# Block attention into a gelu MLP on one core: attention steps 13 to 17 in three batches instead of five

## The chip, the core and the metric

The kernel runs on one core of one Trainium2 chip. The metric is the device time of one execution in microseconds. Before the change it is 199.8 us, the median of three runs (199.78 to 200.85). The profile of one execution has a span of 198.3 us, and that run took 200.1 us, so about 1.8 us of a run lie outside the profiled span.

Names used below: PE is the TensorE, DVE the VectorE, ACT the ScalarE, POOL the GpSimd engine; SP is the engine whose queue starts nearly all transfers.

## The reference, cut to what matters

A causal attention with a per-head decay, computed in blocks of 64 positions with a running 64x64 state per head, and on its output a two-layer MLP with a tanh gelu. Batch 4, 8 heads, 768 positions, head size 64; 3072 tokens of width 512, hidden width 2048.

```python
for b in range(nb):                       # 12 blocks of 64 positions
    intra = einsum('bhic,bhjc->bhij', qb, kb) * Dmask
    intra = einsum('bhij,bhjd->bhid', intra, vb)
    inter = einsum('bhid,bhde->bhie', qb * lam_pow, kv_state)
    out[:, :, sl] = intra + inter
    kv_state = lam_block * kv_state + einsum('bhsd,bhse->bhde', kb * rev_pow, vb)
x = out.transpose(0, 2, 1, 3).reshape(3072, 512)
h = x @ w_in
g = 0.5 * h * (1 + tanh(c * (h + 0.044715 * h**3)))
result = g @ w_out
```

## The kernel before: the parts that the change touches

The attention is cut into 24 steps. A step is 256 positions (a super-block) of four of the eight heads: steps 2m and 2m+1 are the two head halves of super-block m, and three super-blocks make one batch entry. The MLP takes the super-blocks in seven groups, `[[0, 1], [2], [3], [4, 5], [6, 7], [8, 9], [10, 11]]`. Group 3 holds steps 8 to 11, group 4 steps 12 to 15, group 5 steps 16 to 19.

The work of a group is put as small pieces into a list, the filler, when its last attention step has been evacuated. One piece of group 3 is four matmuls of 512 columns with their gelu on ACT, or one of the later products of 8 or 16 smaller matmuls. `fill(n)` issues the next n pieces. So PE alternates between attention steps and runs of MLP pieces, and the program order on every engine is pinned to the order of the calls.

The pools that count here:

```python
ld   = tile_pool(name="ld", bufs=4)      # q, k, v as loaded, fp32
a16p = tile_pool(name="a16", bufs=5)     # q and k in one fp16 tile, v in another
qkp  = tile_pool(name="qkp", bufs=4)     # q and k transposed
ptp  = tile_pool(name="ptp", bufs=3)     # masked scores
ps_M = tile_pool(name="psM", bufs=8, space=PSUM)   # every PSUM tile, one tag
```

Preparing a step: a cast of q times its decay on DVE, a cast of k on ACT, a transpose of both by DMA from SP (from step 9 on), a cast of v on POOL, and then the loads of the step three further on.

```python
def prep_qk(s):
    q32, k32, _ = ld32[s]
    tqk = a16p.tile([P, 2, 2, HH, D], FP16, tag="qk16", ...)
    ...
    pin(q_eng.tensor_tensor(wide(tq), q32[:], decay(dq, s), ALU.mult))   # DVE
    ...
    pin(nc.scalar.activation(out=wide(tk), in_=k32[:], func=AF.Copy))    # ACT
    a16[s] = (tq, tk)
    if s >= FIRST_DMA_T:
        o = qkp.tile([P, 2, 2, 2, P], FP16, tag="qkT", ...)
        pin(nc.sync.dma_start_transpose(out=o..., in_=tqk...))           # SP
        qkT[s] = o
        ...

def prep_v(s):
    tv = a16p.tile([P, 2, HH, D], FP16, tag="v16", ...)
    pin(nc.gpsimd.tensor_tensor(wide(tv[:]), ld32[s][2][:], decay(dv, s), ALU.mult))
    ...
    if s >= 6:
        ...load_ahead(s + 3)                 # q, k, v of step s+3, from SP

def prep(s):
    prep_qk(s)
    prep_v(s)
```

A single step: `R(n, s)` takes the scores of step n (S, 16 matmuls in 64x64 tiles of PE, from the transposed q and k), its keys times values (K, 16 matmuls in 64x64 tiles, 8 in the last super-block of a batch entry), the output of the earlier step s (O, 16 matmuls in 64x64 tiles from the masked scores, and 2 or 4 full-size matmuls with the state u, here called U matmuls). Then ACT copies the output into the MLP's input xT, DVE masks the scores of n, and DVE and POOL advance the state. It takes four PSUM tiles, two for S and two that O and K share (the tiles OK).

```python
def R(n, s, ahead=None):
    if n is not None: scores(n)          # S: 16 matmuls
    if ahead: ahead()
    products(n, s)                       # K: 16 or 8; O: 16; U: 2 or 4; x_out(s) on ACT
    if n is not None: causal(n)          # DVE: PT = S * mask, two instructions
    ...                                  # queue_group when s closes a group
    if n is not None: update(n, 0)       # DVE t, POOL u
def U(n): update(n, 1)                   # the second half of the state update
```

A batch: `burst(ns, ss)` does the same for several steps at once, ordered by kind of matmul. For two steps n it takes all eight PSUM tiles: four S, two O, two K.

```python
def burst(ns, ss, *mix):
    for n in ns: scores(n)
    O = [ps_M.tile([P, 2, 2, P], FP32, tag="M", ...) for c in range(2)]
    for i, s in enumerate(ss): ...       # 16 matmuls O <- PT, v for each s
    K = [ps_M.tile([P, 2, P], FP32, tag="M", ...) for c in range(2)]
    for i, n in enumerate(ns): ...       # 16 or 8 matmuls K <- v, qk for each n
    for i, s in enumerate(ss): ...       # 2 or 4 matmuls O <- qkT, u for each s
    for n in ns: causal(n)
    for i, s in enumerate(ss): x_out(s, ...)
    ...
    if i == len(groups[g]) - 1:
        queue_group(g, *mix)
    for n in ns: update(n, 0)
```

The schedule before: steps 8 to 17 one at a time, and from 18 on in pairs. `sum_win` is one of eight DVE sums of quarters of the first weight matrix, used from about 135 us on.

```python
FILL = {8: (0, 2, 1, 2), ..., 12: (0, 2, 1, 3),
        13: (0, 2, 1, 3), 14: (0, 3, 1, 3), 15: (0, 2, 1, 3), 16: (0, 2, 1, 3), 17: (0, 3, 1, 3)}
for n, (a, b, c, d) in FILL.items():
    stage_t(n)                 # nothing for n >= 9
    fill(a)
    prep_qk(n + 2) if n == 8 else prep(n + 2)
    fill(b)
    R(n, n - 1)
    fill(c)
    U(n)
    ...
    if n == 17:
        prep_qk(20); fill(1); prep_qk(21); fill(1); prep_v(20); prep_v(21); fill(1)
    else:
        fill(d)
    if 8 < n < 17:
        sum_win((n - 7) // 2, (n - 1) % 2, nc.vector)
burst((18, 19), (17,))
fill(2); U(18); U(19); fill(4); prep_qk(22); fill(2)
burst((20, 21), (18, 19), 11, 4)
...
```

Of the kernel before, what the change touches and what calls it, by code (L numbers as in the profile page):

```python
# [15 lines left out]
def kernel(  # L16
# [10 lines left out]
    nc = tc.nc  # L27
# [108 lines left out]
    def w_in_block(t, cs, fs):  # L136

        if t in I_SUMS:
            return wi_sum[(t - 1) // 2][:, (t - 1) % 2, cs, fs]
        F, C = t  # L140
        return w_in16[:, 2 * C + cs.start : 2 * C + cs.stop,
                      F * DFF // 2 + fs.start : F * DFF // 2 + fs.stop]

    def sum_win(m, j, eng):

        if not wi_sum:
            wi_sum.extend(wst.tile([P, 2, 2, DFF // 2], FP16, tag=f"w{2 + i}", name=f"ws{i}")
                          for i in range(2))
        a, op, b = I_SUMS[m]
        cs, fs = slice(0, 2), slice(512 * j, 512 * j + 512)  # L150
        pin(eng.tensor_tensor(w_in_block(m, cs, fs), w_in_block(a, cs, fs),
                              w_in_block(b, cs, fs), op))
# [17 lines left out]
    def load_ahead(s):  # L170
        if s < NSTEP:
            load_step(s)
# [50 lines left out]
    def odd(hs):  # L223
        pin(nc.vector.tensor_tensor(dq[:, hs, 1], dq[:, hs, 0], lam_bc[:, hs], ALU.mult))

    def inverse(hs):
        pin(nc.vector.reciprocal(dv[:, hs], dq[:, hs]))
# [17 lines left out]
# [4 lines that stand above are left out]
    def wide(t):  # L249
        return t.rearrange("p j h d -> p h j d")  # L250

    def decay(t, s):
        hs = halves[s % 2]
        return t[:, hs, :].unsqueeze(3).to_broadcast([P, HH, 2, D])

    def prep_v(s):
        tv = a16p.tile([P, 2, HH, D], FP16, tag="v16", name=f"v16_{s}")
        pin(nc.gpsimd.tensor_tensor(wide(tv[:]), ld32[s][2][:], decay(dv, s), ALU.mult))  # L258
        a16[s] = a16[s] + (tv,)
        if s >= 6:  # L260
            if s + 3 == FIRST_DMA_T + 1:
                load_step(s + 3, "qk")
            else:
                load_ahead(s + 3)

    def prep_qk(s):
        q32, k32, _ = ld32[s]
        tqk = a16p.tile([P, 2, 2, HH, D], FP16, tag="qk16", name=f"qk16_{s}")
        tq, tk = tqk[:, 0], tqk[:, 1]
        q_eng = nc.gpsimd if s == 3 else nc.vector  # L270
        pin(q_eng.tensor_tensor(wide(tq), q32[:], decay(dq, s), ALU.mult))  # L271
        if s == 0:
            inverse(halves[0])
            odd(halves[1])
            inverse(halves[1])
        pin(nc.scalar.activation(out=wide(tk), in_=k32[:], func=AF.Copy))  # L276
        a16[s] = (tq, tk)
        if s >= FIRST_DMA_T:
            o = qkp.tile([P, 2, 2, 2, P], FP16, tag="qkT", name=f"qkT_{s}")
            pin(nc.sync.dma_start_transpose(out=o[:].rearrange("p a j h t -> p (a j h) t"),  # L280
                                            in_=tqk[:].rearrange("p a j h d -> p (a j h d)")))
            qkT[s] = o
            if s == FIRST_DMA_T:
                load_step(s + 1, "v")
# [31 lines left out]
    def half64(i):  # L316
        return slice(64 * i, 64 * i + 64)
# [74 lines left out]
    def burst(ns, ss, *mix):  # L392


        for n in ns:
            scores(n)
        O = [ps_M.tile([P, 2, 2, P], FP32, tag="M", name=f"O{c}") for c in range(2)]
        seen = set()

        def start(kind, c, hl):  # L400
            new = (kind, c, hl) not in seen
            seen.add((kind, c, hl))
            return new

        qTs = [qkT.pop(s) for s in ss]
        for i, s in enumerate(ss):
            PT, tv = PTs.pop(s), a16.pop(s)[2]
            for hp in range(2):
                for jk in range(2):
                    for c, hl in TILES:  # L410
                        pin(nc.tensor.matmul(
                            O[c][half64(hl), i, hp, :], tv[half64(c), jk, 2 * hp + hl, :],
                            PT[half64(c), hl, hp, jk, :], start=start("O", c, hl), stop=False,
                            skip_group_check=True))
        if ns:
            K = [ps_M.tile([P, 2, P], FP32, tag="M", name=f"K{c}") for c in range(2)]
        for i, n in enumerate(ns):
            _, tk, tv = a16[n]
            last = (n // 2) % NSB == NSB - 1
            for jk in range(2):  # L420
                for hp in range(2):
                    for c, hl in TILES:
                        if c == 1 and last:
                            continue
                        pin(nc.tensor.matmul(
                            K[c][half64(hl), i, hp * D : hp * D + D],
                            tk[half64(c), jk, 2 * hp + hl, :], tv[half64(c), jk, 2 * hp + hl, :],
                            start=start("K", c, hl), stop=(jk == 1), skip_group_check=True))
            Kps[n] = [t[:, i] for t in K]
        for i, s in enumerate(ss):  # L430
            for c in range(2):
                if c == 0 and (s // 2) % NSB == 0:
                    continue
                u = us.pop((s, 0) if c else (s - 2, 1))
                for hp in range(2):
                    pin(nc.tensor.matmul(O[c][:, i, hp, :], u[:, hp].rearrange("p l d -> p (l d)"),  # L436
                                         qTs[i][:, 0, :, hp, half64(c)], start=False, stop=True,
                                         skip_group_check=True))
        for n in ns:
            causal(n)  # L440
        for i, s in enumerate(ss):
            x_out(s, [t[:, i].rearrange("p h t -> p (h t)") for t in O])
        sbg = ss[-1] // 2
        g, i = group_of[sbg]
        if i == len(groups[g]) - 1:
            queue_group(g, *mix)
        for n in ns:
            update(n, 0)
# [59 lines left out]
    groups = [[0, 1], [2], [3], [4, 5], [6, 7], [8, 9], [10, 11]]  # L508
# [3 lines left out]
    def queue_group(g, lead=0, per_set=0):  # L512
# [69 lines left out]
        def product(m, p, part=None):  # L582
# [34 lines left out]
            def out_tile(T):  # L617
                if f"o{T}" not in st:
                    st[f"o{T}"] = otp.tile([P, NP, 2, HE], FP32, tag="o32", name=f"o{T}")
                return st[f"o{T}"]  # L620
# [4 lines left out]
            def store(T, ps=slice(0, NP), es=slice(0, 2)):  # L625
                r = row0 + T * HN
                rows = out[r : r + HN, :].rearrange("(p q) (e d) -> q p e d", q=P, e=2)
                whole = g == 3 or (g, T) == (4, 0)
                for i in [ps] if whole else [slice(i, i + 1) for i in range(ps.start, ps.stop)]:
                    pin(nc.sync.dma_start(out=rows[:, i, es], in_=out_tile(T)[:, i, es, :]))  # L630

# [223 lines left out]
    def fill(n):  # L855
        for _ in range(min(n, len(filler))):
            filler.pop(0)()

    def R(n, s, ahead=None):

        if n is not None:
            scores(n)
        if ahead:
            ahead()
        products(n, s)
        if n is not None:
            causal(n)
        if s is not None and s % 2 == 1:
            g, i = group_of[s // 2]
            if i == len(groups[g]) - 1 and g > 0:  # L870
                queue_group(g)
        if n is not None:
            update(n, 0)

    def U(n):
        update(n, 1)
# [17 lines left out]
    idle(2)  # L894
    stage_t(2)
    prep_qk(3)
    update(1, 0)
    update(1, 1, "t")
# [41 lines left out]
    for m in W_SUMS:  # L940
# [29 lines left out]
    prep_v(9)  # L970
    fill(2)

    FILL = {8: (0, 2, 1, 2), 9: (2, 2, 1, 2), 10: (0, 1, 1, 3), 11: (0, 2, 1, 2), 12: (0, 2, 1, 3),
            13: (0, 2, 1, 3), 14: (0, 3, 1, 3), 15: (0, 2, 1, 3), 16: (0, 2, 1, 3), 17: (0, 3, 1, 3)}
    for n, (a, b, c, d) in FILL.items():
        stage_t(n)
        fill(a)
# [4 lines that stand above are left out]
        U(n)  # L982
        if n == 8:
            prep_v(n + 2)
        if n == 17:
            prep_qk(20)
            fill(1)
            prep_qk(21)
            fill(1)
            prep_v(20)  # L990
            prep_v(21)
            fill(1)
        else:
            fill(d)
        if 8 < n < 17:
            sum_win((n - 7) // 2, (n - 1) % 2, nc.vector)

    burst((18, 19), (17,))
    fill(2)
    U(18)  # L1000
    U(19)
# [47 lines left out]
```

## Time and profile before

| | |
|---|---|
| median of three runs | 199.8 us |
| span of the profiled execution | 198.3 us |
| PE busy | 191.9 us (97%) |
| DVE busy | 151.8 us (77%) |
| ACT busy | 123.0 us (62%) |
| POOL busy | 73.6 us (37%) |

The page of a profile gives the busy time of each engine, the span in 40 slices, and the chain of work that ended last: from the last instruction back, at each step to what released it or to what stood before it on its engine. Where a stretch of that chain is PE alone, PE set the pace there. The chain can also be listed in order of time, each piece with its start, its length, its engine and line and the number of instructions. The timeline lists the instructions of an engine with their start and duration, and in brackets the idle time before them with what ended it. The transfers have a time from issue to landing.

Where the steps stand in time, from the starts of the S matmuls in that chain: R(12, 11) at 81.06 us, R(13, 12) at 87.28, R(14, 13) at 94.24, R(15, 14) at 100.35, R(16, 15) at 106.62, R(17, 16) at 113.75, the batch of 18 and 19 at 118.22, that of 20 and 21 at 126.59.

### The profile page before, as it was taken

Reading aid. Unit: us, or ns where it says so; the run is one execution under the profiler, and the core shown is the slowest. Engines: PE = TensorE matmul, PEld = TensorE weight load, DVE = VectorE, ACT = ScalarE, POOL = GpSimd, SP = SyncE. Lnnn points to the kernel's source line nnn. Section 1 sums busy time; section 2 is a strip of 40 time slices with the busy share of each in tenths; the row PEclk is TensorE's granted clock in tenths of the full one; section 3 lists DMA queues with packets and bytes.
Section 4 is the critical chain, followed back from the end, with each engine's and each line's share of the span. In section 5 each row is a group of like instructions: output and inputs, shape, how many; then the busy total and the mean of one; then the engine's idle time right before and its main releaser. Section 6 shows DMA issues by size and latency. Waiting matters only on the chain.

```text
span 198.3 us, 5936 instructions
## 1 busy us (share of the span) xinstructions
PE 191.9 (97%) x2437; PEld 139.7 (70%) x2439; DVE 151.8 (77%) x296; ACT 123.0 (62%) x251; POOL 73.6 (37%) x85
## 2 busy tenths in 40 slices
PE   8879999999999999999999999999999999999993
PEld 2546544456887888754588755578888888888883
DVE  4887722789989989949899378999678997588720
ACT  3673878466693675577745486754668835778321
POOL 6594223456456652436433565047002030002000
PEclk9999999999999999999999999999999999999999
DMA  6999999999999999999864999320211200020205
GB/s 171 291 324 386 386 386 387 292 289 295 293 297 257 217 293 215 210 317 219 226 142 104 271 286 214 106 56 0 53 37 72 105 9 0 0 108 1 106 3 212
DMA packets 61706, 37.86 MB, mean 191 GB/s; under 512 B 17520, under 2 KB 54640, under 8 KB 61680
## 3 DMA queue, kind: packets, MB, share of 16 engines
q1 hardware_dynamic: 61136, 37.23, 71.8%
q8 instruction: 19, 0.31, 0.7%
q10 hardware_dynamic: 544, 0.26, 0.5%
q14 instruction: 7, 0.06, 0.1%
HBM read 27.26 MB, written 6.29 MB: 169 GB/s over the span
## 4 chain that ended last, share of the span: by engine, by line
PE 88%; SPq 4%; DMA 4%; ACT 1%; issue 1%
PE Hps L529 24%; PE MX L606 17%; PE MY L606 9%; PE HX L698 7%; PE O2ps L544 7%; PE MW L606 4%; DMA wi<-in_moe_w_in_dram 4%; SPq L70 4%; PE HY L698 4%; PE S L327 3%; PE Hps L789 3%; PE OK L385 2%; PE HW L698 2%; PE OK L376 2%; PE Tps L298 1%; PE O L436 1%
## 5 line engine op out<-in xcount | busy, mean ns | idle before, releaser
L529 PE MATMUL Hps<-xT,w_in 128*128 128x512 f16 (+1 forms) x288 | 51.0, 332 | 0.0
L488 POOL TENSOR_TENSOR u<-t,lumask 128x256 f16<-128x256 f32 x40 | 29.6, 752 | 49.7 <-DVE t L481 34.1
L529 PEld LDWEIGHTS <-w_in 128*128 128x128 f16 x288 | 27.8, 98 | 18.8
L533 ACT ACTIVATE gT<-Hps 128x512 f16<-128x512 f32 x56 | 32.9, 597 | 10.3 <-PE Hps L529 9.8
L337 DVE TENSOR_TENSOR PT<-S,mask 128x512 f16<-128x512 f32 x48 | 30.5, 682 | 7.4 <-PE S L327 7.3
L606 PEld LDWEIGHTS <-gs 128*128 128x128 f16 x320 | 31.1, 98 | 4.0 <-DVE gs L576 0.4
L258 POOL TENSOR_TENSOR v<-v,dv 128x512 f16<-128x512 f32 x24 | 29.9, 1249 | 7.3 <-DMA v<-in_v_dram 6.9
L606 PEld LDWEIGHTS <-gT 128*128 128x128 f16 x240 | 23.2, 98 | 3.5 <-ACT gT L533 0.5
L606 PE MATMUL MX<-w_sum,gs 128*128 128x256 f16 x160 | 21.5, 273 | 0.0
L271 DVE TENSOR_TENSOR qk<-q,dq 128x512 f16<-128x512 f32 x23 | 19.1, 835 | 1.1 <-DMA q<-in_q_dram 1.0
L576 DVE TENSOR_TENSOR gs<-gT 128x1024 f16<-128x1024 f16 (+1 forms) x24 | 18.4, 772 | 1.6 <-ACT gT L533 1.6
L276 ACT ACTIVATE qk<-k 128x512 f16<-128x512 f32 x24 | 15.0, 626 | 6.9 <-DMA k<-in_k_dram 6.7
L651 POOL TENSOR_TENSOR o<-u,q 128x512 f32<-128x512 f32 (+1 forms) x5 | 5.4, 1082 | 37.2 <-ACT u L623 37.2
L462 ACT ACTIVATE xT<-OK 128x256 f16<-128x256 f32 x34 | 13.0, 454 | 6.3 <-PE OK L385 6.0
L544 PE MATMUL O2ps<-w_out,gT 128*128 128x512 f16 x64 | 14.6, 379 | 0.0
L698 PEld LDWEIGHTS <-ws 128*128 128x128 f16 x128 | 12.5, 98 | 1.8
L623 ACT ACTIVATE u<-MX 128x256 f32<-128x256 f32 x18 | 6.9, 384 | 10.1 <-PE MX L606 10.1
L481 DVE SCALAR_TENSOR_TENSOR t<-t,lamu,OK 128x64 f32<-128x64 f32 x48 | 11.0, 274 | 1.4 <-issue 0.5
L327 PEld LDWEIGHTS <-qkT 64*64 64x64 f16 x384 | 6.1, 106 | 7.1 <-issue 3.4
L544 PEld LDWEIGHTS <-gT 128*128 128x128 f16 x64 | 6.1, 98 | 6.6
L606 PE MATMUL MY<-w_out,gs 128*128 128x256 f16 x80 | 10.7, 273 | 0.0
L606 PE MATMUL MX<-w_sum,gT 128*128 128x256 f16 x80 | 10.4, 273 | 0.0
(95 smaller groups left out, 311.6 us busy)
## 6 DMA issues: line engine op xcount, KB each, us to landing
q<-in_q_dram SPq DMA_DIRECT2D x24, 256.0 KB, 5.0
k<-in_k_dram SPq DMA_DIRECT2D x24, 256.0 KB, 5.1
v<-in_v_dram SPq DMA_DIRECT2D x23, 256.0 KB, 5.4
out_dram<-o SPq DMA_DIRECT2D x17, 256.0 KB, 4.1
wo<-in_moe_w_out_dram SPq DMA_DIRECT2D x4, 1024.0 KB, 9.5
wi<-in_moe_w_in_dram SPq DMA_DIRECT2D x4, 512.0 KB, 8.0
wi<-in_moe_w_in_dram SPq DMA_DIRECT2D x2, 1024.0 KB, 12.7
out_dram<-o SPq DMA_DIRECT2D x3, 512.0 KB, 5.0
```

What stands on the lines that cost most here:

```text
L258: pin(nc.gpsimd.tensor_tensor(wide(tv[:]), ld32[s][2][:], decay(dv, s), ALU.mult))
L271: pin(q_eng.tensor_tensor(wide(tq), q32[:], decay(dq, s), ALU.mult))
L276: pin(nc.scalar.activation(out=wide(tk), in_=k32[:], func=AF.Copy))
L337: pin(nc.vector.tensor_tensor(t[:, hl].rearrange("p b c d -> p b (c d)"), Sps[:].rearrange("p b c d -> p b (c d)"), mask[:].unsqueeze(1).t ...
L462: pin(nc.scalar.activation(out=d, in_=o, func=AF.Copy))
L488: pin(nc.gpsimd.tensor_tensor(u[:], state[half][:].unsqueeze(2).to_broadcast([P, 2, 2, D]), lumask[:, 2 * half : 2 * half + 2, :].unsqueez ...
L529: pin(nc.tensor.matmul(by_block(Hps[:, i, :]), w_in16[:, c, f * P : (f + 1) * P], x(c), start=(c == 0), stop=(c == NC - 1)))
L533: pin(nc.scalar.activation(out=dst, in_=Hps[:], func=AF.Gelu_apprx_tanh))
L544: pin(nc.tensor.matmul(O2[tau][0][:], gT[:, f % HF, f // HF, tau * P : (tau + 1) * P], w_out16[:, f, :], start=(n == 0), stop=(n == NF - 1)))
L576: pin(nc.vector.tensor_tensor(g_rows(m, i), g_rows(a, i), g_rows(b, i), op))
L606: pin(nc.tensor.matmul(dst, lhsT, rhs, start=(opens and i == 0), stop=(closes and i == HF - 1), skip_group_check=True))
L698: pin(nc.tensor.matmul(dst[:, i, :], w_in_block(a, slice(c, c + 1), slice(f * P, f * P + P))[:, 0], x_block(b, slice(c, c + 1))[:, 0], sta ...
```

## The change

The five calls R(13, 12) to R(17, 16) and the batch (18, 19) with output 17 become three batches and one single step: burst (13, 14) with output 12, burst (15, 16) with outputs 13 and 14, R(17, 15), and burst (18, 19) with outputs 16 and 17. It is for fewer changes of PE between MLP matmuls and attention matmuls. The number of filler pieces between R(12, 11) and the batch of 18 and 19 stays 36.

Since step 16 is now wanted soon after step 14, its casts of q and k are made before the first batch. Its transpose needs the place of step 12's transposed tile (four places, steps 12 to 15 hold them), which is read until the end of that batch, and so is issued after it. The last four weight sums on DVE move behind R(17, 15). One store that was a single transfer of 512 KB becomes two of 256 KB.

```diff
     def prep_qk(s):
+        cast_qk(s)
+        transpose_dma(s)
+
+    def cast_qk(s):
         ...
         a16[s] = (tq, tk)
+        whole_qk[s] = tqk
+
+    whole_qk = {}
+
+    def transpose_dma(s):
+        tqk = whole_qk.pop(s)
         if s >= FIRST_DMA_T:
         ...
-        if i == len(groups[g]) - 1:
+        if ss[-1] % 2 == 1 and i == len(groups[g]) - 1:
             queue_group(g, *mix)
         ...
-                whole = g == 3 or (g, T) == (4, 0)
+                whole = g == 3
         ...
-    FILL = {8: ..., 12: (0, 2, 1, 3),
-            13: (0, 2, 1, 3), 14: (0, 3, 1, 3), 15: (0, 2, 1, 3), 16: (0, 2, 1, 3), 17: (0, 3, 1, 3)}
+    FILL = {8: ..., 12: (0, 2, 1, 3)}
     for n, (a, b, c, d) in FILL.items():
         ...
-        if n == 17:
-            ...
-        else:
-            fill(d)
-        if 8 < n < 17:
+        fill(d)
+        if n > 8:
             sum_win((n - 7) // 2, (n - 1) % 2, nc.vector)
 
-    burst((18, 19), (17,))
+    prep(15)
+    fill(1)
+    cast_qk(16)
+    fill(1)
+    burst((13, 14), (12,))
+    transpose_dma(16)
+    fill(1)
+    U(13)
+    U(14)
+    prep_v(16)
+    fill(6)
+    burst((15, 16), (13, 14))
+    fill(1)
+    U(15)
+    U(16)
+    prep(17)
+    fill(8)
+    prep(18)
+    R(17, 15)
+    fill(1)
+    U(17)
+    fill(1)
+    sum_win(3, 0, nc.vector)
+    fill(2)
+    prep(19)
+    sum_win(3, 1, nc.vector)
+    fill(2)
+    sum_win(4, 0, nc.vector)
+    fill(2)
+    sum_win(4, 1, nc.vector)
+    fill(2)
+    prep_qk(20)
+    fill(1)
+    prep_qk(21)
+    prep_v(20)
+    fill(3)
+
+    burst((18, 19), (16, 17))
+    prep_v(21)
     fill(2)
     U(18)
     U(19)
```

More of the change, by code (lines that the diff above doesn't have):

```diff
@@ L971 @@
     fill(2)
-    FILL = {8: (0, 2, 1, 2), 9: (2, 2, 1, 2), 10: (0, 1, 1, 3), 11: (0, 2, 1, 2), 12: (0, 2, 1, 3),
-            13: (0, 2, 1, 3), 14: (0, 3, 1, 3), 15: (0, 2, 1, 3), 16: (0, 2, 1, 3), 17: (0, 3, 1, 3)}
+    FILL = {8: (0, 2, 1, 2), 9: (2, 2, 1, 2), 10: (0, 1, 1, 3), 11: (0, 2, 1, 2), 12: (0, 2, 1, 3)}
     for n, (a, b, c, d) in FILL.items():
@@ L984 @@
             prep_v(n + 2)
-        if n == 17:
[L986 to L992, printed above, removed]
-        else:
-            fill(d)
-        if 8 < n < 17:
-            sum_win((n - 7) // 2, (n - 1) % 2, nc.vector)
-    burst((18, 19), (17,))
+        fill(d)
+        if n > 8:
+            sum_win((n - 7) // 2, (n - 1) % 2, nc.vector)
+    prep(15)
[36 more added lines that the diff above has]
+    prep_v(21)
     fill(2)
```

## The prediction

> **What bounds the kernel now.** I read the page first, for the engine that fills the span:
>
> ```profile
> span 198.3 us, 5936 instructions
> PE 191.9 (97%) x2437; PEld 139.7 (70%) x2439; DVE 151.8 (77%) x296; ACT 123.0 (62%) x251; POOL 73.6 (37%) x85
> PE 88%; SPq 4%; DMA 4%; ACT 1%; issue 1%
> ```
>
> PE is busy for 97% of the span and makes 88% of the chain that ended last. A busy PE can hide waits, so I went on to the chain in order of time (start, length, what), for the stretch that the change rewrites. First one single step, R(13, 12), with the filler run behind it; then the two batches that exist already:
>
> ```profile
> 87.28 0.35 PE S L327 x16
> 87.63 0.12 PE OK L362 x16
> 87.75 0.23 PE OK L376 x16
> 87.98 0.22 PE OK L385 x2
> 88.19 6.04 PE Hps L529 x28
> ...
> 118.22 0.57 PE S L327 x32
> 118.80 0.22 PE O L411 x16
> 119.02 0.33 PE K L425 x32
> ...
> 126.59 0.57 PE S L327 x32
> 127.16 0.45 PE O L411 x32
> 127.60 0.28 PE K L425 x32
> 127.88 0.33 PE O L436 x4
> ```
>
> The pieces join without a gap, and 28 matmuls in 6.04 us is 0.216 us each, the rate of the long runs everywhere. So between 81 and 128 us PE waits for nothing: time can be won here only by giving PE less to do, and any new wait of PE is lost in full. The lines also price the steps. The first 16 S cost 0.35 us, the next 16 only 0.22: 0.13 is the price of entering. Two U matmuls cost 0.22 and four 0.33: 0.055 each and 0.11 of entering. O and K show hardly any such part.
>
> Then the things that PE could come to wait for. ACT just ahead of R(13, 12) (start, duration), the SP queue behind it (start, issue time), and landings of a load of v and of the transpose of step 16:
>
> ```profile
> 86.08 0.62 ACT L276 ACTIVATE qk<-k 128x512 f16<-128x512 f32 x1
> 86.60 1.31 ACT L533 ACTIVATE gT<-Hps 128x512 f16<-128x512 f32 x2
> ```
> ```profile
> 86.73 2.16 SPq L280 DMA_TRANSPOSE qkT<-qk  x1
> 88.94 0.57 SPq L70 DMA_DIRECT2D q<-in_q_dram  x1
> 89.56 0.51 SPq L70 DMA_DIRECT2D k<-in_k_dram  x1
> 90.11 1.14 SPq L70 DMA_DIRECT2D v<-in_v_dram  x1
> 92.83 1.24 SPq L280 DMA_TRANSPOSE qkT<-qk  x1
> ```
> ```profile
> v<-in_v_dram SPq DMA_DIRECT2D x1, 256.0 KB, 5.0
> qkT<-qk SPq DMA_TRANSPOSE x1, 3.2
> ```
>
> ACT finishes the last gelu before R(13, 12) at 87.91, 0.63 us after PE has begun the step; the single step does not need that bank. The SP queue is busy from 86.73 to 91.25 with the transpose of step 15 and the loads of step 18. The v of step 18 lands at 90.11 + 5.0 = 95.1 us, the transpose of step 16 at 92.83 + 3.2 = 96.0.
>
> **What the Trainium skill says.** "TensorEngine Tiling (Array Packing)", section Key Properties: changing the tiling mode drains TensorE. That is the entering cost that batches share, and the trace agrees (0.13 us at S, 0.11 at U). "TensorE: Matmul & The Clock Gate", section Architectural detail, calls ACT and DVE strict FIFO: a cast put before a gelu delays the gelu and the bank it frees. The trace agrees: the gelus start at 86.60, when the cast of k is through. "DMA: Bandwidth & Descriptors", section Queues, rings and completion order: on each DMA engine a queue's descriptors are consumed in ring order, though writes may finish out of order. So a transpose issued behind three loads mostly lands behind them. The trace agrees for step 16 (96.0 after 95.1).
>
> **What the change saves on PE.** No matmul is added or removed: 112 S, 96 O and all K and U stay. Before, from the chain: R(13, 12) and R(14, 13) 0.91 us each (two U), R(15, 14) 1.03, R(16, 15) and R(17, 16) 1.02 each (four U), the batch of 18 and 19 with one output 1.46 (118.22 to the next MLP piece at 119.68). Sum 6.35. After, put together from the lines above:
> - burst (13, 14) with output 12: S 0.57, O 0.22, K 0.28, two U 0.22, sum 1.29.
> - burst (15, 16) with outputs 13 and 14: S 0.57, O 0.45, 24 K about 0.23, six U 0.44, sum 1.69.
> - R(17, 15): 1.02.
> - burst (18, 19) with outputs 16 and 17: S 0.57, O 0.45, K 0.28, eight U 0.55, sum 1.85.
>
> Together 5.85, and so 0.5 us less. Six visits become four, and each visit saved is 0.13 + 0.11 = 0.24 us, which also gives 0.48. I take 0.45, since the 0.33 of K in the first batch may recur.
>
> **What it may cost: a PSUM bank in the first batch.** Two steps in a batch take all eight banks, so the last one, of K, is the bank of the filler piece just ahead of the batch, and frees when ACT has made its gelu. The cast of k of step 16 now stands between the last two gelus. From their lines a gelu occupies ACT about 0.49 us and a cast of k 0.52 (86.08 to 86.60). So: gelu 86.60, cast 87.09, last gelu 87.61 to 88.21, instead of 87.91. PE reaches K at 87.28 + 0.57 + 0.22 = 88.07. Wait: 0.14, with the signal about 0.17 us.
>
> **What it may cost: the transpose of step 16.** It must wait for the end of the first batch, at about 87.28 + 1.29 + 0.17 = 88.74, but SP reaches it only after the loads of step 18, at 91.3. PE wants it early: seven filler pieces at 0.864 make 6.05, so burst (15, 16) starts at 94.79, and the S of step 16 stands at 94.79 + 0.35 = 95.14. If the transpose lands 3.1 us after its issue, the shortest in the trace, it is there at 94.4 and costs nothing. If it follows the v of step 18 at the same distance of 0.9 us as before, it lands at 96.0 and PE waits 0.8. I take the middle, 0.4.
>
> **What I count as hidden.** DVE: at 91.6 us it is through the four masks (2.48 us for four, at the batch of 18 and 19, from 87.67) and the state updates of 13 and 14 (about 1.3), then the four gelu sums of 0.69 bring it to 94.4, before the next scores at 95.1. It fits only because the weight sum of 0.72 us that stood here is moved, and moving it costs nothing: the sums are read from about 135 us. POOL: four state products of about 0.8 and the cast of v of step 16, 1.49, end near 95.1, and K of step 16 comes near 96. The transposes of steps 20 and 21 both wait now for the end of the third batch (near 120), and by the 3.4 us that the second took before they land by 125.5; their S stands at 126.5 or later. Two stores for one is 0.5 us of SP.
>
> Sum: -0.45 + 0.17 + 0.4 = +0.1 us, so 199.9.
>
> **The rivals.** First, everything new is hidden: the transpose lands by 95.1 and the gelu in time. For it: the issue-to-landing time of transposes in an empty queue is 3.1 to 3.2 us, and the change takes care to make the casts of step 16 early. Against it: three loads stand directly ahead. It makes 199.8 - 0.45 = 199.35. Second, the transpose is a new wait in full: 0.8 to 1.5 us, the latter with a landing 5.5 us after issue, like that of step 15 (5.7). For it: every transpose issued right behind loads here took 4.4 us or more. It makes 200.3 to 201.0. Third, DVE becomes the bound: with two steps' masks and updates at once plus the gelu sums, it holds back the scores' banks and so the MLP pieces. Against it: the addition above, with 0.7 us to spare. For it: that addition has DVE never waiting between 87.7 and 94.4. Half a microsecond more, and the effect would be seen at the seventh piece after a batch; it makes 200.3.
>
> **Range and chances.** The saving is sure to within 0.1 us; the waits run from 0 to about 1.5. With a scatter of runs of some 0.3 us I predict 199.9 us, and 199.3 to 200.7 for 8 times in 10. That the change moves the time by over 2% (4 us) either way I hold for nearly excluded, as it touches some 6 us of PE's time: faster 0.005, within 2% 0.985, slower 0.01.
>
> **What would show it.** In the profile after: the four visits near 1.3, 1.7, 1.0 and 1.85 us in the chain; an ACT gelu ahead of K in the first batch as a wait of 0.1 to 0.3; between the first and the second half of S in burst (15, 16) a wait for the transpose of step 16, landing between 94.4 and 96.5, with the issue at 91.3. No PE wait on DVE or POOL from 88 to 118, and none for the transposes of 20 and 21. I am wrong if the visits do not get shorter, if SP gets to the transpose much earlier or later than 91.3, or if waits appear after 97 us.

## The result, and the profile after

The changed kernel takes 201.76 us (median of six runs, 201.29 to 202.40), against 199.82 for the kernel before: a ratio of 1.009, with a 95% interval of 1.0066 to 1.0115. It is slower by about 1.9 us; I had predicted 199.9 with 200.7 as the upper end.

The page of the changed kernel, the same three lines as before:

```profile
span 200.1 us, 5935 instructions
PE 192.3 (96%) x2437; PEld 140.6 (70%) x2439; DVE 153.8 (77%) x296; ACT 122.8 (61%) x251; POOL 73.6 (37%) x85
PE 86%; DMA 6%; DVE 2%; ACT 2%; issue 1%; SPq 1%; POOL 1%; DVEq 0%; POOLq 0%
```

The busy time of PE tells nothing: 192.3 us, as much as before. The chain tells it. DMA has 6% of it now, and one transfer stands in the middle of the stretch that was pure PE. The chain in order of time (start, length, what), from the first batch on; the second block is the list of PE's waits (total, times, longest), two of its lines. Hps is the first product of an MLP piece and gT its gelu; MX, MY and MW are later MLP products, gs is a DVE sum of gelu tiles, PT are the masked scores:

```profile
87.34 0.52 ACT qk L280
87.85 0.50 ACT gT L543
88.35 0.04 issue
88.39 0.44 PE K L435 x31
88.83 0.22 PE O L446 x2
89.05 2.40 PE Hps L539 x12
91.45 5.49 DMA qkT<-qk
96.94 0.04 issue
96.98 0.42 PE S L337 x16
97.40 0.45 PE O L421 x32
97.85 0.25 PE K L435 x24
98.09 0.44 PE O L446 x6
98.54 3.45 PE Hps L539 x16
...
119.56 0.57 PE S L337 x32
...
121.38 6.91 PE Hps L539 x32
128.29 0.57 PE S L337 x32
```
```profile
PE S L337 <- DMA qkT<-qk: 1.5, 1, 1.5
PE K L435 <- ACT gT L543: 0.2, 1, 0.2
```

Two waits are to be seen, both of the predicted kind. In the first batch K waits for a gelu that ACT could only make after the cast of k of step 16 (the 0.52 ahead of it). In the second, the S of step 16 waits for its transpose, and the two halves of S cost 0.35 and 0.42 us where a joint S costs 0.57: PE pays the entering twice, some 0.2 us. Where the transfer comes from is in the SP queue (start, issue time) and in the landings (the last number, us from issue):

```profile
89.02 0.58 SPq L70 DMA_DIRECT2D q<-in_q_dram  x1
89.64 0.51 SPq L70 DMA_DIRECT2D k<-in_k_dram  x1
90.19 1.09 SPq L70 DMA_DIRECT2D v<-in_v_dram  x1
91.45 1.56 SPq L290 DMA_TRANSPOSE qkT<-qk  x1
```
```profile
v<-in_v_dram SPq DMA_DIRECT2D x1, 256.0 KB, 5.7
qkT<-qk SPq DMA_TRANSPOSE x1, 5.5
```

SP issues the transpose at 91.45, behind the three loads of step 18. The v of step 18 lands at 90.19 + 5.7 = 95.9, the transpose 1.0 us after it, at 96.9. In the kernel before they landed at 95.1 and 96.0, although the transpose was issued 1.4 us later: issuing it earlier behind the same loads brought nothing.

The account of the stretch from R(12, 11) to the batch of 20 and 21: 81.06 to 126.59, 45.53 us, before; 81.21 to 128.29, 47.08, after. So 1.55 us arise here, of the 1.8 by which the two spans differ. The four visits take 1.62, 3.44, 1.02 and 1.82 us, in all 7.90 against 6.35.

### The profile page after: what moved, and what is told of

Read it like the earlier page. It is cut to its first block, busy times and chain, and to the rows that moved or that the text cites. A ratio compares the mean times of both kernels' runs of the same rounds, so it can differ in the third digit from the quotient of the medians.

```text
span 200.1 us, 5935 instructions
## 1 busy us (share of the span) xinstructions
PE 192.3 (96%) x2437; PEld 140.6 (70%) x2439; DVE 153.8 (77%) x296; ACT 122.8 (61%) x251; POOL 73.6 (37%) x85
## 4 chain that ended last, share of the span: by engine, by line
PE 86%; DMA 6%; DVE 2%; ACT 2%; issue 1%; SPq 1%; POOL 1%; DVEq 0%; POOLq 0%
PE Hps L539 21%; PE MX L616 17%; PE MY L616 9%; PE HX L708 7%; PE O2ps L554 7%; PE MW L616 4%; PE Hps L799 4%; PE HY L708 4%; DMA v<-in_v_dram 3%; PE S L337 3%; DMA qkT<-qk 3%; PE HW L708 2%; PE OK L395 2%; PE Tps L308 1%; PE O L446 1%; PE OK L386 1%
## 5 line engine op out<-in xcount | busy, mean ns | idle before, releaser
L586 DVE TENSOR_TENSOR gs<-gT 128x1024 f16<-128x1024 f16 (+1 forms) x24 | 17.2, 723 | 4.2 <-ACT gT L543 4.2
L275 DVE TENSOR_TENSOR qk<-q,dq 128x512 f16<-128x512 f32 x23 | 20.1, 882 | 0.3 <-DMA q<-in_q_dram 0.3
L472 ACT ACTIVATE xT<-OK 128x256 f16<-128x256 f32 x26 | 9.9, 452 | 8.3 <-PE OK L395 8.2
L472 ACT ACTIVATE xT<-O 128x256 f16<-128x256 f32 x22 | 8.0, 460 | 7.7 <-PE O L446 7.1
L337 PE MATMUL S<-qkT 64*64 64x128 f16 x384 | 9.3, 222 | 2.1 <-DMA qkT<-qk 1.5
L586 DVE TENSOR_TENSOR gs<-gs,gT 128x1024 f16<-128x1024 f16 (+1 forms) x12 | 11.1, 923 | 0.3
```

The lines of the kernel that those rows point to most:

```text
L337: pin(nc.tensor.matmul(Sps[hl][half64(c), hp, jk, :], o[half64(hl), 1, jk, hp, half64(c)], o[half64(hl), 0, :, hp, half64(c)], start=True, ...
L472: pin(nc.scalar.activation(out=d, in_=o, func=AF.Copy))
L586: pin(nc.vector.tensor_tensor(g_rows(m, i), g_rows(a, i), g_rows(b, i), op))
```

## The experiments

Theory A: the saving on PE is there, and is lost to the transpose of step 16, which is late because of its place behind the loads of step 18, and a little to the gelu behind the cast. Rivals: B, the transpose is late because it waits for the place that step 12 frees, or is slow anywhere; C, DVE holds PE back as soon as the transfer does not. All edits are to the changed kernel unless said otherwise. In eleven of E5's 22 runs and three of E8's seven the clock of the core was lower (0.991 to 0.992), and the times given for these two leave those runs out; all other medians hold every run.

**E1: the loads of step 18 behind the transpose of step 16.**

```diff
-        if s >= 6:
+        if s >= 6 and s != 15:             # prep_v(15) loads nothing
     ...
     transpose_dma(16)
+    load_ahead(18)
```

> The changed kernel with the three loads of step 18 issued behind the transpose of step 16 instead of ahead of it; nothing else moves. Theory A (the new wait is the place of the transpose in the transfer queue): the transpose is issued near 89.1 us, when the first batch ends, lands by 93.5, the wait of 1.54 us between the two halves of S and the 0.2 us of entering S a second time go, and the time falls from 201.76 to about 200.0; the wait of K for the gelu (0.3 us) stays. Rival B (the transpose waits mostly for the slot that the first batch frees, or takes 5.5 us anywhere): it lands at 94.6 or later and the time falls by at most 0.5 us. Rival C (DVE's work holds back the scores once the transpose does not): the wait for the transpose goes, but waits of PE on DVE of 0.5 us or more take its place, time 200.5 to 201.3.

Measured: 200.14 us, ratio to the kernel before 1.0017 (1.0009 to 1.0025). So 1.6 us of the loss go with the order of four transfers. The transpose is issued at 88.80 instead of 91.45, and PE waits for it no more:

```profile
88.80 2.19 SPq L290 DMA_TRANSPOSE qkT<-qk  x1
```

Its landing is not recorded, but its packets are. Every transpose here moves 1024 packets of 256 bytes, and the last of these ends at 92.52 us, 3.7 us after the issue. So the transpose is not slow wherever it stands, which was one half of rival B. Rival C showed itself too, in a small way. The chain of E1 around the second batch:

```profile
91.86 1.15 DVE gs L586
93.01 0.02 issue
93.03 1.43 DVE gs L586
94.46 0.02 issue
94.48 1.29 DVE gs L586 x2
95.78 0.61 DVE PT L347
96.39 0.04 issue
96.43 3.61 PE Hps L539 x16
```

DVE is at its four gelu sums until 95.78, then makes the first mask of step 15, and the MLP piece behind the batch starts 0.04 us after that mask has freed its bank; its 16 matmuls take 3.61 us instead of 3.45. It costs some 0.2 us, which the late transfer had covered up.

**E2: the casts of steps 15 and 16 one filler piece earlier.**

```diff
-    FILL = {..., 12: (0, 2, 1, 3)}
+    FILL = {..., 12: (0, 2, 1, 2)}
     prep(15)
-    fill(1)
     cast_qk(16)
-    fill(1)
+    fill(3)
     burst((13, 14), (12,))
```

> The changed kernel with the casts of steps 15 and 16 made one filler piece earlier, both together, so that ACT can catch up before the first batch. Theory A: the wait of K for the last gelu (0.3 us) goes, but the transpose of step 16 still lands near 96.9, so PE only waits longer for it (1.8 instead of 1.54 us) and the time stays at 201.6 to 201.9. Rival B (the two waits add): 201.4 or less.

Measured: 201.67 us, ratio 1.0099 (1.0064 to 1.0134). K of the first batch waits no more. But the wait for the transpose is 1.50 us in the trace, not the 1.8 expected: with the casts of step 15 earlier, SP starts earlier too, and the transpose of step 16 lands at 96.67, 0.27 before its time in the changed kernel. The stretch from R(12, 11) to the batch of 20 and 21 is 46.76 us against 47.08. The medians differ by only 0.09 us, but each is of six runs that spread over 1 us or more; whether the edit alone gains 0.3 us or nothing stays open, and rival B is not excluded. In both traces PE goes on 0.04 us after the landing. Two lines of the chain of E2:

```profile
88.27 0.33 PE K L435 x32
...
91.09 5.58 DMA qkT<-qk
```

**E3: both edits.**

> Both edits together: loads of step 18 behind the transpose of step 16, and the casts of steps 15 and 16 one filler piece earlier. Theory A: both waits go, 1.54 + 0.2 + 0.3 us, and what is left is the saving of the shorter visits: 201.76 - 2.05 = 199.7, or 199.35 if the 0.3 us outside the rewritten stretch are noise of the profile. That is 0 to 0.5 us under the kernel before. Rival C (DVE): 200.2 or more with waits of PE on DVE.

Measured: 199.85 us, ratio 0.9993 (0.9973 to 1.0012): the kernel before, not better. The edit of E2 is worth 0.29 us here (200.14 to 199.85), and the stretch agrees (45.58 us in E1, 45.30 here). The wait on the mask is as in E1 (the MLP piece starts at 96.42, again with 3.61 us).

**E4: nine MLP pieces between the first two batches instead of seven.**

```diff
     prep_v(16)
-    fill(6)
+    fill(8)
     burst((15, 16), (13, 14))
     ...
     prep(17)
-    fill(8)
+    fill(6)
     prep(18)
```

> The changed kernel with two of the MLP pieces moved from behind the second batch to ahead of it (9 pieces between the first two batches instead of 7); the transfers keep their order. Theory A: the second batch comes 1.73 us later on PE, near 96.8, the transpose still lands near 96.9, the wait of 1.54 us shrinks to 0 to 0.3, and the time is 200.0 to 200.3, as with the loads behind the transpose. Rival B (something other than the landing sets the second batch): the wait moves along with the batch, time 201.3 or more.

Measured: 200.95 us, ratio 1.0055 (1.0027 to 1.0082), with runs from 199.93 to 202.72. The wait for step 16's transpose fell to 0.20 us in the profiled run, whose span was 198.5 us, as theory A has it; this is PE there:

```profile
96.42 0.42 PE L337 MATMUL S<-qkT 64*64 64x128 f16 x16
97.03 0.42 PE L337 MATMUL S<-qkT 64*64 64x128 f16 x16 [0.20 <-DMA qkT<-qk]
```

But the median missed the expected 200.0 to 200.3. In the same trace the S of step 17 comes just as its transpose lands, 101.3 + 3.4 = 104.7 us. The two pieces taken from behind the second batch are missing there as time for step 17. Two landings on the edge would also explain the wide scatter; the longer runs have no trace, so that is argued, not shown.

**E5: as E3, and two of the four gelu sums moved behind the second batch.**

```diff
-            behind(9, 0, 4, (1, 2, 4, 3))
+            if g == 3:
+                behind(9, 0, 4, (1, 2))
+                behind(12, 0, 4, (4, 3))
+            else:
+                behind(9, 0, 4, (1, 2, 4, 3))
```

> The kernel with both edits, and in addition two of the four gelu sums that DVE makes between the first two batches moved behind the second batch. In the trace with both edits these four sums took 0.85, 0.99, 1.41 and 0.68 us, 3.9 in all instead of the 2.8 I had counted, the masks of step 15 began only at 95.69 (S stood ready near 95.0), and the first MLP piece after the batch started at 96.42 on a bank that a mask had just freed, with 3.61 us for 16 matmuls instead of 3.45. Theory A' (DVE's sums are what is left of the saving): masks begin at 95.0, the piece starts by 96.3 and takes 3.45, and the time is 0.2 to 0.3 us below that with both edits: 199.5 to 199.65, under the kernel before. Rival (nothing is left of that kind, the rest of the saving is lost in the scatter of the transfers): 199.85 again.

Measured: 201.82 us, ratio 1.0059 (1.0027 to 1.009); three of the eleven runs lie at 199.80 to 200.21, eight at 201.46 to 202.77. My expectation failed as to the time. The profiled run is one of the long ones (202.77), and its chain says why:

```profile
97.12 3.45 PE Hps L539 x16
100.58 1.55 PE MX L616 x15
102.13 4.89 DMA qkT<-qk
107.02 0.04 issue
107.06 0.42 PE S L337 x16
```

The columns are start, length and what. The part the edit aimed at is repaired: the piece behind the second batch takes 3.45 us. But the moved sums now stand on DVE ahead of the cast of q of step 17, which ran at 101.31, and so its transpose was issued at 102.13, 1.3 us later than in E3 if both are counted from R(12, 11), and PE waited 2.1 us for it. Only part of this wait is the late issue. In E3 that transpose landed 3.1 us after its issue; had it done so here, PE would have waited 0.3 us. It took 4.9. The last of its packets ends at 104.90 us, where a packet of instructions of 16 KB begins, and the landing follows at 107.02; beside the transpose of E3 there is no such packet. So the late issue took the slack away and a slow landing made most of the wait. Landings of 3.1 us would explain the three short runs; they have no trace, so this is argued, not shown.

**E6: as E3, with one of the moved weight sums back between the batches.**

```diff
     prep_v(16)
-    fill(6)
+    fill(3)
+    sum_win(3, 0, nc.vector)
+    fill(3)
     burst((15, 16), (13, 14))
     ...
-    sum_win(3, 0, nc.vector)
```

> The kernel with both edits, but one of the moved weight sums (0.7 us on DVE) put back between the first two batches, where it stood before the change. Theory A' (DVE between the batches is full and on the edge): masks of step 15 begin 0.7 us later, near 96.4, the MLP pieces after the second batch wait for their banks by some 0.7 us more, time 200.4 to 200.7. Rival (DVE has slack, moving the sums was not needed): 199.85.

Measured: 200.31 us, ratio 1.0011 (0.9992 to 1.003); 0.46 above E3, a little less than expected. PE's waits have a new line:

```profile
PE Hps L539 <- DVE PT L347: 0.5, 1, 0.5
```

So the move of the sums in the change is needed: 0.7 us more on DVE at this place costs about half a microsecond.

**E7: a fifth place for transposed tiles, the transpose of step 16 issued with its casts.**

```diff
-    qkp = ... bufs=4        # and ubp bufs=4
+    qkp = ... bufs=5        # and ubp bufs=3, for the room
     cast_qk(16)
+    transpose_dma(16)
     fill(1)
     burst((13, 14), (12,))
-    transpose_dma(16)
```

> The changed kernel with five places for transposed tiles instead of four, and the transpose of step 16 issued with its casts, ahead of the first batch in program order; the loads of step 18 still stand ahead of it in the transfer queue. (To make room, the state tiles u have three places per half instead of four.) Theory A (the queue order sets the landing): SP still comes to the transpose only near 91.3, it lands near 96.9, time 201.6 to 201.9. Rival B (the transpose waits for the place that step 12 frees): issue before 89, landing by 94.5, time near 200.1.

Measured: 202.12 us, ratio 1.010 (1.0056 to 1.0144), of four runs and 0.2 above the expected range. Without the wait for step 12's place the transpose is still issued at 91.04 and lands 5.6 us later:

```profile
91.04 5.57 DMA qkT<-qk
```

So the other half of rival B falls: the place was free in time, the queue was not.

**E8: the split store of group 4 made whole again.**

```diff
-                whole = g == 3
+                whole = g == 3 or (g, T) == (4, 0)
```

> The changed kernel with the one store of group 4 that was split made whole again. All theories: no difference, 201.6 to 201.9; the store leaves near 114.5 us, when no transfer is waited for. If it were part of the loss, the time would fall by more than 0.2 us.

Measured: 201.95 us (four runs, 201.56 to 202.55). The time did not fall, so the store is no part of the loss.

**E9: as E5, with the casts of step 17 between the first two batches and its transpose ahead of the loads of step 20.**

```diff
-        if s >= 6 and s != 15:
+        if s >= 6 and s not in (15, 17):
     ...
-    fill(6)
+    fill(2)
+    cast_qk(17)
+    fill(4)
     burst((15, 16), (13, 14))
+    transpose_dma(17)
+    load_ahead(20)
     ...
-    prep(17)
+    prep_v(17)
```

> The kernel with both edits and the split gelu sums, and the casts of step 17 made between the first two batches, its transpose issued right behind the second batch with the loads of step 20 behind it. In the trace with the split sums the first two batches ran in 1.34 and 1.70 us without a wait, but the cast of q of step 17 then stood behind the moved sums, its transpose was issued at 102.1 and landed at 107.0, and PE waited 2.1 us for it. Theory A (transposes that come late are all that stands against the saving): issue near 96.3, landing by 101, no wait of PE on a transfer or on DVE between 87 and 120 us; the four visits take 1.34, 1.70, 1.02 and 1.85, 0.44 less than the 6.35 of before: 199.4 to 199.6, under both kernels. Rival D (the saving is eaten by something that no wait shows): 199.8 or more with no wait in the trace.

Measured: 199.59 us, ratio 0.9986 (0.9974 to 0.9997), faster than both kernels; the kernel before took 199.87 in the runs beside it, 0.28 more. The chain of E9 through the batches is PE alone:

```profile
86.96 0.57 PE S L337 x32
87.53 0.22 PE O L421 x16
87.76 0.33 PE K L435 x32
88.09 0.22 PE O L446 x2
88.31 6.04 PE Hps L539 x28
94.35 0.57 PE S L337 x32
94.92 0.45 PE O L421 x32
95.37 0.25 PE K L435 x24
95.61 0.44 PE O L446 x6
96.06 3.45 PE Hps L539 x16
```

The four visits take 1.35, 1.71, 1.02 and 1.82 us: 5.90, which is 0.45 less than before. The stretch from R(12, 11) to the batch of 20 and 21 is 45.06 us, against 45.53 before. Why the time falls by 0.28 us and the stretch by 0.47 is not shown.

**E10: as E9, but the four gelu sums not split.**

> As before, but the four gelu sums not split: 0.7 us more on DVE between the first two batches than in the kernel with both edits, and the transpose of step 17 early. Theory A' (DVE is on the edge there): PE waits on DVE's masks after the second batch by 0.4 to 0.7 us, time 200.2 to 200.5, as with the weight sum put back. Rival: 199.85 or less.

Measured: 200.27 us, ratio 1.0013 (1.0004 to 1.0022). PE waits 0.5 us for the masks, as in E6. So both parts of E9 are needed: the early cast alone overfills DVE between the batches, and the split alone makes the next transpose late (E5).

## Why the prediction was wrong

**The saving on PE was right.** I had summed the four visits to 5.85 us and taken 0.45 us as the gain. E9, with no wait left in these visits, shows 5.90 and 0.45.

**The step that failed is the cost of the transpose of step 16, counted as 0.4 us, the middle of 0 and 0.8.** The mechanism was the predicted one, and the issue time nearly so (91.3 predicted, 91.45 measured). The size was wrong: 1.54 us of waiting and about 0.2 of entering S a second time, 1.74 in all. With it the terms of my sum read -0.45 + 0.27 + 1.74 = 1.56 us, and the four visits did become 1.55 us longer. Three things went into it:
- I should not have averaged. The lower end, 3.1 us to landing, I had read from transposes issued 1.6 us or more after the transfer ahead of them, and even of these one took 4.9 us (issued at 128.18 in the kernel before). Every trace here that keeps the loads of step 18 directly ahead has the transpose landing 5.5 to 5.6 us after its issue (the changed kernel, E2, E4, E7, E8). My second rival took just such a line, the transpose of step 15, and its upper end, a wait of 1.5 us, is what came.
- Even my upper end of 0.8 was low, since I took the landing of the v of step 18 from the kernel before as fixed. It came 0.8 us later, at 95.9. In the changed kernel the DMA engines move some 20 GB/s instead of 280 from 94.9 to 95.7 us, in the middle of this transpose, and that v lands just behind the gap. E2, E4, E7 and E8 have a gap of 0.8 to 0.9 us in the same place; the kernel before, with 1.6 us between the loads and the transpose, has none there. What makes the gap is open.
- PE came to ask at 95.45 us (the second batch starts at 95.10), 0.3 later than the 95.14 predicted, 0.15 of it already there at R(12, 11). That made the wait shorter, not longer, and I had no term for entering S twice.

**The cost of the gelu behind the cast, 0.17 us, was 0.27** (1.62 us for the first visit against 1.35 in E9); E1 and E3 differ by 0.29. The mechanism held: the wait itself is 0.15 us, and K, one matmul of which stands ahead of the wait, takes 0.44 us behind it instead of 0.33. But my sum added two waits that stood one behind the other ahead of the same landing. As long as the landing does not move, a shorter first wait only makes the second longer. That is argued from the chain; E2 does not show it, as its landing moved too.

**DVE, which I held to be hidden with 0.7 us to spare, was hidden only as long as the transfer was late.** I counted each gelu sum as 0.69 us. Between the batches four of them took 3.9 us in the trace of E3. "SBUF — State Buffer" of the Trainium skill, section Terms, says that DVE and GpSimd arbitrate for one pair of ports and that the loser blocks fully. The traces fit: in E1 the first two sums, under POOL's state products and cast of v, took 1.14 and 1.42 us, and the last two, with POOL idle, 0.69 each; the cast of v ended at 93.90 and the second sum 0.55 us after it. DVE also stood 0.67 us ahead of the first sum, waiting for a gelu, which I had not counted. The row that I took from the kernel before has both kinds of sums in it; I read off the short ones. In the changed kernel PE's wait for the transfer lay over all this, and so it is no part of its 1.9 us.

**The rest held**: POOL, the transposes of steps 20 and 21, the split store. Some 0.25 us of the 1.8 between the two spans lie outside the rewritten stretch; 0.15 stand ahead of it, where the two programs do the same. Their cause is open.

So the change is sound as an idea and lost in a detail: the transpose was made early on every engine except the queue that issues it.

## What to carry to other kernels

When work is pulled forward, look at the one queue that issues its transfers: a transfer that is wanted soon goes ahead of the loads that have time, and its landing is read from transfers with the same things ahead of them, not from the shortest in the trace. Do not add up waits that end at the same landing. When a wait goes, ask each engine again what it hides: here three in a row stood behind one another (transfer, masks on DVE, the next transfer), and the 0.45 us came out of PE's visits only when all were gone, with 0.28 us of it in the time.

## What the runs showed that I had not expected

A transpose of 256 KB between SBUF tiles landed 5.5 to 5.6 us after its issue directly behind the three loads of step 18. With nothing issued for 2.4 us or more ahead of it, it landed after 3.0 to 3.4 us or after 4.5 to 4.9. In all twelve traces there are 58 such transposes: the 33 without a 16 KB packet of instructions between issue and landing took 3.1 to 3.4 us, and 22 of the 25 with one took 4.5 to 4.9. That the packet is the cause is not shown.

DVE sums of two 16-bit tiles of 128 x 1024 took 0.69 us alone and up to 1.53 beside POOL. Splitting one visit of PE's small tiles by a wait costs some 0.2 us on top of the wait at S, and 0.11 at K.
